# Stage B's score fills regrouped over both row halves of the array, and a changed rule for filling gaps in a planned schedule

## The chip, the cores and the metric

The kernel runs on one core of one Trainium2 chip. The metric is device time of the whole program in microseconds (us), the median of several runs. A core has five engines with queues of their own, which run in order and wait for one another by semaphores: TensorE (PE in the profile, with its weight loads as PEld), VectorE (DVE), ScalarE (ACT), GpSimd (POOL) and SyncE (SP, which here issues most of the transfers). TensorE's results go to tiles in PSUM, which this kernel allots in banks of 512 float32 columns in 128 partitions; ScalarE and VectorE read them there.

## What is computed

Two stages, one after the other, for each of 8 batches of 448 tokens.

```python
# stage A: attention of 12 heads of 64, with a soft cap on the scores
scores = cap * np.tanh(scale * (q @ k.T) / cap)      # cap = 30
attn = softmax(scores)
x = attn @ v                                         # 12 heads side by side: 768 columns
# stage B: 4 experts, each a causal attention of one head of 64 over x
logits = x @ w_gate                                  # each token takes its 2 best experts
for e in range(4):
    qe, ke, ve = x @ wq[e], x @ wk[e], x @ wv[e]
    a = softmax(where(causal, scale * (qe @ ke.T)))
    out += weight[:, e] * (a @ ve @ wo[e])           # weight is 0 where e isn't chosen
```

## The kernel before

**Tiling.** Heads go in pairs: two heads of 64 fill the 128 rows of the array, head 0 in rows 0 to 63 and head 1 in rows 64 to 127. There are 48 pairs, six to a batch. Scores stand transposed (keys in partitions, queries in columns), so that they serve as weights for the product with the values. The 448 keys are three chunks of 128 and a tail of 64. In stage B the experts go in pairs too, r = 0 for experts 0 and 1, r = 1 for 2 and 3; inside a pair the expert is e = 0 or 1 (also called g), with its `qe` and `ke` in rows 64e to 64e + 63.

**Stage A of a pair.** Four fills (`fill`, L444) put the scores of a chunk for both heads into a score buffer; the fourth, with the tails, is a single matmul of all rows (L449). ScalarE reads each by a tanh (`tanh`, L462, the instruction is L467): three of 896 columns and one of 448, called T0 to T3. Two exps (`expo`, L472; L474) follow on the tanh results, E0 of 1792 and E1 of 1344 columns. Then `a_pv_mm` multiplies by the values (L497 and L491, four parts in a plan), VectorE divides, and a transpose (`a_xt_tr`, L536) makes the batch's `xT`.

**Stage B of a batch.** Once the six pairs of a batch are in `xT`, the projections q, k (`b_qk`, in three parts of two matmuls) and v (`b_v`, in two) follow, then for each pair r two fills `b_fill(b, r, g)` (L675) and two exps `b_exp(b, r, g)` (L697, ScalarE at L703), named X0 and X1 below. Each works on a part of the score columns: before the change part g holds expert e = g, and part 0 has the tails of both experts besides. Causality cuts the blocks: chunk c of keys needs queries from 128c on, so its block has 448, 320 or 192 columns; the tail has 64. `COL` gives each block's column in the exp tile `pB`, which begins with 64 columns of zeros. After the exp GpSimd clears the upper triangle of each block on the diagonal (`affine_select`, L711). `b_pv` multiplies with the values for one expert, `b_ot` transposes, `b_wo` projects and `b_store` writes out.

**Two score buffers.** `ps_score` has two buffers of 1024 float32 (two banks each). T and X fills take turns in the order `reads`, so a fill may start when the ScalarE instruction two places earlier has read its buffer. Other PSUM tiles come from four single banks (`ps_aux`).

**The order of the work.** ScalarE's order is written out in `prog` (L894): for pair p it is T0, T1, E1 of the pair before, T2, T3, E0. In 14 of the 48 slots (`EXPB`, L891: two for each of the batches 0 to 6) stage B of an earlier batch comes in: T0, T1, X0, E1, X1, T2, T3, E0. TensorE's order comes from a planner, `Plan` (L18), which runs when the program is built and has no part in its execution. It keeps a clock for TensorE, VectorE and ScalarE; a unit of work has an estimated duration, dependencies and a due time. Before each fill, `do_fill` (L920) asks the planner to fill TensorE's time (`pump`, L86): no unit starts after `until`, when the fill's buffer comes free, and none is to end after `latest`, which is the time at which ScalarE will want the fill, less the fill's cost and 0.4 us. `step` (L65) finds the earliest possible start among the ready units, takes from those within 0.3 us of it the one that is due first, and emits it; in the kernel before, if that one doesn't end by `latest`, nothing more is placed in this gap. Some estimated durations: a half of `pv` 0.235 us (two parts make 0.47), `xt` 0.22, a part of `v` 0.33, of `q` or `k` 0.377, the transposes of a new pair (`tr`) 0.43, `pvB` 0.31, `wo` 0.33.

**The end.** The last batch, with whatever is left in the plan, is ordered by another planner (`last_batch`, L1026; `Graph.solve`, L150): a list schedule improved by 4000 random trials with a fixed seed, from the planner's clocks at that point.

Of the kernel before, what the change touches and what calls it, by code (L numbers as in the profile page):

```python
# [17 lines left out]
class Plan:  # L18
# [46 lines left out]
    def step(self, until, latest):  # L65


        at = {}
        for u in self.work:
            r = self.ready(u)  # L70
            if r is not None:
                at[u["key"]] = max(r, self.pe)
        if not at:
            return False
        first = min(at.values())
        u = min(
            (u for u in self.work if at.get(u["key"], 1.0e9) <= first + 0.3),
            key=lambda u: u["due"],
        )
        if first > until or first + u["pe"] > latest:  # L80
            return False
        self.work.remove(u)
        self.emit(u)
        return True
# [156 lines left out]
def kernel(  # L241
# [24 lines left out]
    KC, KM = 3, 384  # L266
# [403 lines left out]

    COL = {(0, 0): 64, (0, 1): 512, (0, 2): 832, (1, 1): 1024, (1, 2): 1344, (1, 0): 1536}

    def b_fill(b, r, g):  # L675
        s = st[b]
        qe = s["qe", r]
        ke = s["ke", r]
        sc = ps_score.tile([128, 1024], f32, name=f"sB{g}_{b}_{r}", tag="score")

        def block(e, o, ko, n, to):

            h = slice(64 * e, 64 * (e + 1))
            nc.tensor.matmul(  # L684
                sc[to : to + n, o : o + S - ko], ke[h, ko : ko + n], qe[h, ko:S], start=True,
                stop=True,
            )

        if g == 0:
            for e in range(2):  # L690
                block(e, 0, KM, TL, 64 * e)
        for (e, c), o in COL.items():
            if e == g:
                block(e, o - 1024 * g, 128 * c, 128, 0)
        s["sc", r, g] = sc

    def b_exp(b, r, g):  # L697

        assert b < 2 or ("pvB", b - 2, E - 1) in plan.done
        pb = pB[2 * (b % 2) + r]  # L700
        n = 1024 - 64 * g
        o0 = 64 + 1024 * g
        nc.scalar.activation(  # L703
            pb[:, o0 : o0 + n], st[b].pop(("sc", r, g))[:, 0:n], AF.Exp, scale=isc
        )
        blocks = [(o, 0, 128, 128) for (e, _), o in COL.items() if e == g]
        if g == 0:
            blocks += [(0, 0, 64, 64), (0, 64, 128, 64)]
        for o, r0, r1, n in blocks:
            blk = pb[r0:r1, 64 + o : 64 + o + n]  # L710
            nc.gpsimd.affine_select(  # L711
                out=blk, in_=blk, compare_op=ALU.is_ge, fill=0.0, base=0,
                pattern=[[1, n]], channel_multiplier=-1,
            )

    def b_pv_mm(b, e):
# [4 lines left out]
        for n in range(4):  # L721
            w = WIN[n]
            ops = []
            for c in range(KC):
                if 128 * c <= w:
                    ops.append((64 + COL[(g, c)] + w - 128 * c, s["vall"][:, c, e, :]))
            if n == 3:
# [182 lines left out]
    def dur(o):  # L910
        if o[0] == "S":
            return 0.0
        if o[0] == "X":
            return 0.9
        return 0.09 + 0.373 * (4 - o[2]) if o[0] == "E" else 0.055 + 0.373 * HALF[o[2]]

    def fill_dep(o):
        return (("tr", o[1]),) if o[0] == "T" else (("q", o[1], o[2]), ("k", o[1], o[2]))

    def do_fill():  # L920
        nonlocal nfill
        o = reads[nfill]
        rel = ends[nfill - 2] if nfill >= 2 else 0.0
        cost = 0.55 if o[0] == "X" else 0.5 if o[2] < KC else 0.19
        for d in fill_dep(o):
            plan.force(d)
        at = plan.act + sum(dur(x) for x in prog[pos : where[nfill]])
        plan.pump(rel, at - cost - 0.4)
        plan.pe = max(plan.pe, rel, *(plan.done[d] for d in fill_dep(o))) + cost
        fill(*o[1:]) if o[0] == "T" else b_fill(*o[1:])  # L930
        plan.done[("f", nfill)] = plan.pe + plan.LAT
        nfill += 1
# [10 lines left out]
    def slot(p):  # L943
# [24 lines left out]
        if p >= HP and p % HP == 0 and p < NP:  # L968
            batch(p // HP - 1)
# [10 lines left out]
    def batch(b):  # L980
        x = ("xt", HP * b + HP - 1)
        t0, t1 = nom["X", b, 0, 0], nom["X", b, 1, 0]
        for r, t in enumerate((t0, t1)):
            plan.parts(("q", b, r), 3, 1.13, 0.55, [x, ("w", ("q", r))], t - 4.0, b_qk, b, r, "q")
            plan.parts(("k", b, r), 3, 1.13, 0.55, [x, ("w", ("k", r))], t - 4.0, b_qk, b, r, "k")
        for n in range(4):
            d = [("v", b, n - 1)] if n else [x, ("w", "v")]
            plan.parts(("v", b, n), 2, 0.66, 0.6, d, t0 + 2.0 * n, b_v, b, n)
        plan.add(("g1", b), 0.0, 1.0, [("v", b, 3)], t1 + 1.0, b_gate, b, aux=None)
        plan.add(("g", b), 0.0, 0.8, [("g1", b), ("G", b)], t1 + 3.0, b_gate2, b, aux=None)  # L990
        for e in range(E):
            due = t1 + 6.0 + 3.0 * e
            d = [("X", b, e // 2, e % 2), ("g", b)] + [("pvB", b, e - 1)] * (e % 2)
            plan.add(("pvB", b, e), 0.31, 0.7, d, due, b_pv, b, e)
            if e % 2:
                plan.add(("oT", b, e // 2), 0.22, 0.35, [("pvB", b, e)], due, b_ot, b, e // 2)
        for n in range(4):
            for f in range(2):
                i = 2 * n + f
                d = [("oT", b, 1), ("w", "o")] if i == 0 else [("wo", b, *divmod(i - 1, 2))]  # L1000
                due = t1 + 19.0 + 1.5 * i
                plan.add(("wo", b, n, f), 0.33, 0.5, d, due, b_wo, b, n, f)
# [23 lines left out]
    def last_batch():  # L1026


        p, b = NP - 1, B - 1
        c = b - 1  # L1030
# [22 lines left out]
        BOTH = ("aux", "tail")  # L1053
# [4 lines left out]
        def op(key, eng, deps, fn, *args, group=None, groups=(), opens=None):  # L1058
            after = max([plan.done[d] for d in deps if d in plan.done], default=0.0)
            groups = (group,) if group else groups  # L1060
            f = (lambda e: fn(*args, e == "ACT")) if len(eng) > 1 else (lambda e: fn(*args))
            bias = 0.0
            if key[0] == "qk":
                bias = BR * (key[1] == 0)
            elif key[0] in ("pvL", "otL"):
                bias = BA * (key[1] == "A")
            elif key[0] == "sL":
                bias = BA * (key[1][0] == "A")
            elif key[0] in ("wo", "st"):
                bias = BA * (key[1] == b and key[2] < 2) - BW * (key[1] == c)  # L1070
            elif key[0] in ("pv", "xtp", "xt"):
                bias = BX
            G.op(key, eng, deps, f, groups, opens, after, bias)


        for u in (p - 1, p):
            for i in range(2):
                if ("pv", u, i) not in left and u < p:
                    continue
                g = ("pv", u, i)  # L1080
# [9 lines left out]
            g = ("xtp", u)  # L1090
# [18 lines left out]
        for e in range(E):  # L1109
            if ("pvB", c, e) in left:  # L1110
                g = ("pvB", c, e)
                r = e // 2
                op((*g, 0), {"PE": 0.31}, [("X", c, r, e % 2)], b_pv_mm, c, e, group=g, opens=BOTH)
                op((*g, 1), {"DVE": 0.18}, [(*g, 0)], b_pv_rc, c, e, group=g)
                op((*g, 2), {"DVE": 0.17}, [(*g, 1), ("gate", c, 8), ("g", c)], b_pv_sl, c, e)
                d = [(*g, 2)] + [("pvB", c, e - 1, 3)] * (e % 2)
                op((*g, 3), {"DVE": 0.43}, d, b_pv_osc, c, e, group=g)
        for r in range(2):
            if ("oT", c, r) in left:
                g = ("oT", c, r)  # L1120
                d = [("pvB", c, 2 * r + 1, 3)]
# [25 lines left out]
        for n in range(4):  # L1147
            for f in range(2):
                if ("wo", c, n, f) in left:
                    d = [[("oT", c, 0), ("oT", c, 1)]]  # L1150
# [42 lines left out]
        for r in range(2):  # L1193
            for w in "qk":
                g = ("qk", r, w)
                for j in range(NDC):
                    if (*g, j) in plan.done:
                        G.held[g] = "aux"
                        continue
                    d = [("xt", x0 + j)] + [(*g, j - 1)] * (j > 0)  # L1200
                    op(
                        (*g, j), {"PE": 0.19}, d, qk_mm, r, w, j, group=g,
                        opens=None if j else BOTH,
                    )
                d = [(*g, NDC - 1)] + [("el", NDC - 1)] * (r == 1 and w == "q")
                op((*g, "out"), both(0.6, 0.53), d, q_out if w == "q" else k_out, r, group=g)
        g = ("qk", 1, "q")
        for j in range(NDC):
            d = [("xt", x0 + j), (*g, 0)] + [("el", j - 1)] * (j > 0)
# [4 lines left out]
        for m in range(2):  # L1214
            g = ("vl", m)
            prev = None
            for j0, j1 in ((0, 3), (3, 5), (5, 6)):
                for i in range(2):
                    d = [("xt", x0 + j1 - 1), prev or ("xtp", p, 0)]
# [3 lines left out]
                        opens=BOTH if i + j0 == 0 else None,  # L1223
# [46 lines left out]
        for x, (blocks, o0) in BANKS.items():  # L1270
            rs = {a[0] for a in blocks}
            for e in range(2):
                o = o0 + (320 if x[0] == "C" else 384) * e
                for r, k0, q0, q1 in blocks:
                    if x[0] == "C" and k0 == TAIL:
                        o = o0 + 320 * e
# [4 lines left out]
            g = [("sL", x, e) for e in range(2)]  # L1281
# [4 lines left out]
            for e in range(2):  # L1286
                op(
                    ("sL", x, e), {"ACT": 0.49 if x[0] == "C" else 0.38}, [("sL", x, "mm")],
                    exps, x, e, group=g[e],
# [58 lines left out]
        for q in "AB":  # L1348
            need = {"A": (0,), "B": (0, 1)}[q]
            for r in range(2):  # L1350
                g = ("pvL", q, r)
                d = done[q, r] + [("vl", m, "out") for m in need]
# [8 lines left out]
            for n in (0, 1) if q == "A" else (2, 3):  # L1361
                for f in range(2):
                    d = [[("otL", q, r, 1)] for r in range(2)]
# [90 lines left out]
```

The softmax here doesn't subtract the row's maximum and nothing guards it: scores larger than these inputs give would overflow.

## Time and profile before

| what | value |
|---|---|
| time, median of 3 runs | 332.28 us (332.13 to 333.07) |
| span of the profiled execution | 330.7 us |
| mean granted TensorE clock | 0.984 |
| first tanh / end of the last exp of stage A | 8.23 us / 309.2 us |
| 144 tanh of 896 columns, mean | 978 ns |
| 48 exp of 1792, 48 exp of 1344, mean | 1762 ns, 1370 ns |
| 14 exp of 1024, 14 exp of 960 of stage B, mean | 1023 ns, 962 ns |
| 112 matmuls of stage B's scores | 18.3 us busy |

A row of the profile's groups gives the line, engine, operation and tile, the shape and count, then the busy time in us with the mean of one in ns, and behind the second bar the time for which its engine was idle just before, with what ended it. The timeline gives start and length in us; instructions of one line that follow each other are merged and counted (x5). Neighbouring records on one engine can overlap: a tanh of 978 ns is followed by the next after 797 ns. So the pace of ScalarE is read from start to start, not from the lengths.

### The profile page before, as it was taken

To read this page: it belongs to the slowest core of one execution; us is meant where nothing else is said; L and a number is where in the kernel's file an instruction comes from. 1 tells how busy PE (TensorE), PEld (TensorE's weight loads), DVE (VectorE), ACT (ScalarE), POOL (GpSimd) and SP (SyncE) were. 2 spreads that over 40 slices of the span, in tenths; PEclk is the share of its full clock that TensorE was granted. 3 is DMA by queue.
4 is the path that set the end of the run, shared out by engine and by line. 5 is a ranking of instruction groups with operands and counts; after the bars stand their busy time and mean duration, and the time that the engine had idled before them with its cause. 6 is when DMAs were issued, how large, how long until landed. Compare 5 with 4: busy or idle time off the path is not lost.

```text
span 330.7 us, 8813 instructions
## 1 busy us (share of the span) xinstructions
PE 279.7 (85%) x3335; PEld 177.4 (54%) x3335; DVE 212.2 (64%) x745; ACT 312.0 (94%) x353; POOL 156.0 (47%) x476
## 2 busy tenths in 40 slices
PE   5486589977889988998899889998798898898992
PEld 2254365555456564556655566556555565555861
DVE  4255445576557786668956688568855686646682
ACT  2989999999999999999999999999999999999592
POOL 3489999456707299765805285173912020022000
PEclk9999979999999999999999999999999999999997
DMA  7899999950363999477074903577003101120017
GB/s 165 214 247 246 216 222 233 211 116 3 87 177 88 285 264 258 145 195 179 3 217 158 287 13 108 156 216 192 3 7 138 24 3 50 50 71 3 2 74 261
DMA packets 65146, 46.19 MB, mean 140 GB/s; under 512 B 25872, under 2 KB 61584, under 8 KB 65104
## 3 DMA queue, kind: packets, MB, share of 16 engines
q1 hardware_dynamic: 54032, 43.58, 51.1%
q0 software_dynamic: 10512, 1.58, 6.7%
q8 instruction: 26, 0.43, 0.5%
q10 hardware_dynamic: 560, 0.48, 0.5%
q14 instruction: 16, 0.13, 0.1%
HBM read 36.19 MB, written 11.01 MB: 143 GB/s over the span
## 4 chain that ended last, share of the span: by engine, by line
ACT 81%; PE 7%; DMA 5%; POOL 3%; issue 1%; SPq 1%; DVEq 0%; ACTq 0%; POOLq 0%; DVE 0%
ACT y L467 38%; ACT p L474 35%; ACT pBs L703 8%; DMA ktf<-in_k_dram 3%; DMA kf<-in_k_dram 2%; PE wops L785 2%; POOL pBs L711 1%; PE vps L567 1%; PE kps L648 1%; PE qps L648 1%; POOL q L393 1%; PE pv L497 1%; POOL k L390 0%; POOL ktzs L389 0%; PE pvB L730 0%
## 5 line engine op out<-in xcount | busy, mean ns | idle before, releaser
L467 ACT ACTIVATE y<-s 128x896 f16<-128x896 f32 x192 | 152.7, 883 | 2.2 <-PE s L449 1.1
L474 ACT ACTIVATE p<-y 128x1792 f16<-128x1792 f16 x96 | 150.0, 1566 | 0.0
L711 POOL TENSOR_SCALAR_AFFINE_SELECT pBs<-pBs 128x128 f16<-128x128 f16 (+1 forms) x112 | 27.8, 278 | 123.6 <-ACT pBs L703 122.7
L453 PE MATMUL s<-qt,kt 64*128 64x448 f16 x288 | 52.5, 370 | 18.8 <-ACT y L467 14.5
L497 PE MATMUL pv<-v16s,p 128*128 128x65 f16 x1152 | 62.4, 196 | 5.9 <-ACT p L474 5.1
L497 PEld LDWEIGHTS <-p 128*128 128x128 f16 x1152 | 52.5, 99 | 24.7 <-issue 10.1
L453 PEld LDWEIGHTS <-kt 64*128 64x128 f16 x288 | 18.1, 94 | 47.8 <-issue 38.1
L511 DVE TENSOR_TENSOR xk<-pv,rc 128x256 f16<-128x256 f32 x96 | 40.6, 424 | 3.2
L491 PE MATMUL pv<-vtzs,p 128*128 128x130 f16 x192 | 42.0, 222 | 0.0
L507 DVE RECIPROCAL rc<-pv 128x4 f32<-128x4 f32 x96 | 17.1, 180 | 37.9 <-PE pv L491 37.0
L372 DVE COPY ob<-wops 128x384 f32<-128x384 f32 (+1 forms) x55 | 30.5, 554 | 9.1 <-PE wops L785 8.4
L785 PE MATMUL wops<-wo,oT 128*128 128x384 f16 x128 | 30.2, 326 | 0.0
L567 PE MATMUL vps<-wvg,xT 128*128 128x260 f16 (+1 forms) x192 | 29.8, 275 | 0.0
L703 ACT ACTIVATE pBs<-sB 128x1024 f16<-128x1024 f32 (+1 forms) x28 | 27.8, 992 | 0.7
L393 POOL CAST q<-qf 112x512 f16<-112x512 f32 x46 | 27.9, 607 | 0.0
L390 POOL CAST k<-kf 128x384 f16<-128x384 f32 x48 | 24.1, 502 | 6.8 <-DMA kf<-in_k_dram 3.9
L389 POOL CAST ktzs<-ktf 64x64 f16<-64x64 f32 x92 | 21.3, 232 | 9.1 <-DMA ktf<-in_k_dram 3.9
L684 PE MATMUL sB<-qe,ke 64*128 64x192 f16 (+2 forms) x112 | 18.3, 274 | 8.3 <-ACT y L467 4.7
L401 POOL CAST v16s<-vf 128x384 f16<-128x384 f32 x48 | 24.5, 510 | 1.2 <-DMA vf<-in_v_dram 1.0
L648 PE MATMUL qps<-xT,wq 128*128 128x448 f16 x96 | 24.9, 354 | 0.0
L648 PE MATMUL kps<-xT,wk 128*128 128x448 f16 x96 | 24.8, 353 | 0.0
L431 DVE COPY qt<-tps 128x384 f16<-128x384 f16 x48 | 16.8, 351 | 12.3 <-PE tps L421 12.3
(120 smaller groups left out, 456.7 us busy)
## 6 DMA issues: line engine op xcount, KB each, us to landing
qf<-in_q_dram SPq DMA_DIRECT2D x23, 448.0 KB, 5.6
out_dram<-ob SPq DMA_DIRECT2D x24, 384.0 KB, 2.9
kf<-in_k_dram SPq DMA_DIRECT2D x23, 384.0 KB, 6.4
vf<-in_v_dram SPq DMA_DIRECT2D x23, 384.0 KB, 5.8
ktf<-in_k_dram SPq DMA_DIRECT2D x46, 32.0 KB, 5.5
vtf<-in_v_dram SPq DMA_DIRECT2D x46, 32.0 KB, 5.1
out_dram<-ob SPq DMA_DIRECT2D x7, 192.0 KB, 2.9
qf<-in_q_dram ACTq DMA_DIRECT2D x2, 224.0 KB, 4.0
```

Source lines behind the costliest of these rows:

```text
L393: eng.tensor_copy(q16, qf.rearrange("p h (c d) -> p c h d", c=QC))
L453: nc.tensor.matmul(sc[:, g, 0:S], kt[r, 128 * (i + 1) : 128 * (i + 2)], qt[r, :], start=True, stop=True,)
L467: nc.scalar.activation(y[(p, g)][:, 2 * (i % 2) : 2 * (i % 2) + n, :], score.pop((p, i))[:, 0:n, 0:S], AF.Tanh, scale=isc / capf,)
L474: nc.scalar.activation(pt, y.pop((p, g)), AF.Exp, scale=capf)
L491: nc.tensor.matmul(pv[:, n, :, :], pt[:, 2, w : w + 128], vtz[p % 12], start=False, stop=True, skip_group_check=True,)
L497: nc.tensor.matmul(pv[:, n, g, :], pt[:, 2 * (c % 2) + g, w : w + 128], v16[p % 12][:, g, c, :], start=(n == 0 and c == 0 and g == 0), sto ...
L511: nc.vector.tensor_tensor(xt[p][:, 2 * i : 2 * i + 2, :, :], pv[:, :, :, 0:Dh], rc.broadcast_to((128, 2, 2, Dh)), ALU.mult,)
L567: nc.tensor.matmul(ps, xT[b][:, j, w : w + 128], wvg[:, j, 0 : ps.shape[1]], start=(j == 0 and first), stop=(j == NDC - 1), skip_group_che ...
L648: nc.tensor.matmul(ps, w2[r][:, j, :], xT[b][:, j, :], start=(j == 0), stop=(j == NDC - 1), skip_group_check=(b == B - 1),)
L703: nc.scalar.activation(pb[:, o0 : o0 + n], st[b].pop(("sc", r, g))[:, 0:n], AF.Exp, scale=isc)
L711: nc.gpsimd.affine_select(out=blk, in_=blk, compare_op=ALU.is_ge, fill=0.0, base=0, pattern=[[1, n]], channel_multiplier=-1,)
L785: nc.tensor.matmul(ps, st[b]["oT", r][:, w : w + 128], wo2[r][:, f * (D // 2) : (f + 1) * (D // 2)], start=(r == 0), stop=(r == 1),)
```

## The change

Part g of stage B's scores now holds both experts. Part 0 has the two blocks of chunk 0 (448 columns for each expert) and the two tails; part 1 has chunks 1 and 2 of both (320 and 192 columns for each). In each part one expert's blocks lie in the first bank of the score buffer and the other's in the second, and the matmuls of the two experts alternate, so that the two halves of the array's rows can work at once. Part 0 is now 960 columns and part 1 is 1024. The four `pvB` of a batch all wait for X1 of their pair, since X1 holds columns of both experts.

In the planner an X fill is reckoned at 0.45 us instead of 0.55, and `step` considers only units that end by `latest`; before, it chose first and gave up if the choice didn't fit.

```diff
@@ step
-            if r is not None:
+            if r is not None and max(r, self.pe) + u["pe"] <= latest:
                 at[u["key"]] = max(r, self.pe)
...
-        if first > until or first + u["pe"] > latest:
+        if first > until:
             return False
@@ columns
-    COL = {(0, 0): 64, (0, 1): 512, (0, 2): 832, (1, 1): 1024, (1, 2): 1344, (1, 0): 1536}
+    COL = {(0, 0): 64, (1, 0): 512, (0, 1): 960, (0, 2): 1280, (1, 1): 1472, (1, 2): 1792}
+    XCOL = (0, 960, 1984)
@@ b_fill
+        for c in (1, 2) if g else (0,):
+            for e in range(2):
+                block(e, COL[e, c] - XCOL[g], 128 * c, 128, 0)
         if g == 0:
             for e in range(2):
                 block(e, 0, KM, TL, 64 * e)
-        for (e, c), o in COL.items():
-            if e == g:
-                block(e, o - 1024 * g, 128 * c, 128, 0)
@@ b_exp
-        n = 1024 - 64 * g
-        o0 = 64 + 1024 * g
+        n = XCOL[g + 1] - XCOL[g]
+        o0 = 64 + XCOL[g]
...
-        blocks = [(o, 0, 128, 128) for (e, _), o in COL.items() if e == g]
+        blocks = [(o, 0, 128, 128) for (_, c), o in COL.items() if (c > 0) == g]
@@ do_fill
-        cost = 0.55 if o[0] == "X" else 0.5 if o[2] < KC else 0.19
+        cost = 0.45 if o[0] == "X" else 0.5 if o[2] < KC else 0.19
@@ batch
-            d = [("X", b, e // 2, e % 2), ("g", b)] + [("pvB", b, e - 1)] * (e % 2)
+            d = [("X", b, e // 2, 1), ("g", b)] + [("pvB", b, e - 1)] * (e % 2)
@@ last_batch
-                op((*g, 0), {"PE": 0.31}, [("X", c, r, e % 2)], b_pv_mm, c, e, group=g, opens=BOTH)
+                op((*g, 0), {"PE": 0.31}, [("X", c, r, 1)], b_pv_mm, c, e, group=g, opens=BOTH)
```

## The prediction

> **What bounds the kernel now.** I read the page first: busy shares, the chain of waits, the groups.
>
> ```profile
> PE 279.7 (85%) x3335; PEld 177.4 (54%) x3335; DVE 212.2 (64%) x745; ACT 312.0 (94%) x353; POOL 156.0 (47%) x476
> ACT y L467 38%; ACT p L474 35%; ACT pBs L703 8%; DMA ktf<-in_k_dram 3%; DMA kf<-in_k_dram 2%; PE wops L785 2%; POOL pBs L711 1%; PE vps L567 1%; PE kps L648 1%; PE qps L648 1%; POOL q L393 1%; PE pv L497 1%; POOL k L390 0%; POOL ktzs L389 0%; PE pvB L730 0%
> L703 ACT ACTIVATE pBs<-sB 128x1024 f16<-128x1024 f32 (+1 forms) x28 | 27.8, 992 | 0.7
> ```
>
> ScalarE (ACT) is busy for 94% and carries 81% of the chain with three instructions: tanh (L467), exp of stage A (L474), exp of stage B (L703). VectorE, GpSimd and the DMA queues matter only where they hold up ACT. The last row looks as if stage B's exp cost ACT 0.7 us of idle time in all, but records of neighbours on ACT overlap, so a wait can hide in an overlap that is missing. So I went to the timeline, ACT first around one of the 14 places where stage B's exp comes in:
>
> ```profile
> 210.99 1.04 ACT L467 ACTIVATE y<-s 128x896 f16<-128x896 f32 x1
> ...
> 211.79 1.05 ACT L467 ACTIVATE y<-s 128x896 f16<-128x896 f32 x1
> 212.91 1.02 ACT L703 ACTIVATE pBs<-sB 128x1024 f16<-128x1024 f32 x1
> 213.83 1.31 ACT L474 ACTIVATE p<-y 128x1344 f16<-128x1344 f16 x1
> ```
>
> Columns: start, duration. A tanh of 896 is followed by the next instruction after 0.80 (210.99 to 211.79), but the exp of stage B starts 1.12 after its tanh. The 14 starts of a first part (X0) in the timeline lie 1.15, 0.99, 1.07, 0.99, 1.13, 1.05, 1.12, 1.05, 1.12, 1.05, 1.13, 1.05, 1.13, 1.01 after their tanh: 15.02 in all, against 14 x 0.797 = 11.16 without a wait. So **3.87 us** are lost there. The second part (X1) follows the exp of 1344 after 1.21, as a tanh does: nothing is lost. Between 23 and 309 us I find no other stretch of ACT above its floor. What X0 waits for is on TensorE (PE):
>
> ```profile
> 211.45 0.22 PE L532 MATMUL xtp<-pswap,xk 128*128 128x128 f16 x1
> 212.09 0.73 PE L684 MATMUL sB<-qe,ke 64*64 64x64 f16 x5 [0.42 <-ACT y L467]
> 212.75 0.50 PE L785 MATMUL wops<-wo,oT 128*128 128x384 f16 x2
> 213.18 0.58 PE L684 MATMUL sB<-qe,ke 64*128 64x320 f16 x3
> ```
>
> The score buffers are two. The first tanh of the slot ends at 212.03 (210.99 + 1.04) and frees one; PE, idle for 0.42, starts the fill at 212.09, needs 0.73, and ACT starts 0.09 later. 0.24 + 0.06 + 0.73 + 0.09 = 1.12: the whole period is explained by the fill's length. X1's fill of 0.58 has the exp of 1344 beside it.
>
> **What the Trainium skill says.** "TensorEngine Tiling (Array Packing)", Tiling Modes (Key Properties): tiles of the array work independently, so row halves run at once, but a change of mode, not of tile, drains the array. The trace agrees with both. Stage A's fills, one matmul for each half, take 0.36 for the pair, and two pairs 0.55 at the least, so a pair costs about 0.20 where the mode stays:
>
> ```profile
> 58.09 0.59 PE L453 MATMUL s<-qt,kt 64*128 64x448 f16 x4
> 206.44 0.36 PE L453 MATMUL s<-qt,kt 64*128 64x448 f16 x2 [0.31 <-ACT y L467]
> 206.74 0.34 PE L532 MATMUL xtp<-perm,xk 128*128 128x128 f16 x3
> ```
>
> After the lone pair the next operation, of another mode, starts 0.30 later instead of 0.20: a switch costs some 0.10. The same page, Gotcha 1, says that row tiles that run at once must write different banks. That is the new layout: e = 0 in columns 0 to 511 of the buffer, e = 1 in 512 to 1023. No page is needed for the rest.
>
> **The change, part by part.** (1) *First fill.* Inside the old fill the five matmuls start at 0, 0.00, 0.149, 0.349, 0.485 and the last takes 0.243 (the mean of its form): two tails at once (64*64), then 448, 320 and 192 columns one after the other on one half. New: 448 of both halves at once, then the tails of both at once. The pair 448 to the next operation of another mode costs 0.296 (above), the tails take 0.20 (rows of 64x64: 200 ns), so 0.50; ends: 0.41 if the switch to 64*64 drains nothing, 0.73 if the halves did not overlap at all. I take 0.50, as the old fill shows the switch too (0.149 between starts for only 64 columns). It is 0.23 shorter. Taking 0.23 from each of the 14 excesses, none below zero, leaves 0.13, 0.04, 0.10, 0.02, 0.09, 0.03, 0.10, 0.02, 0.10, 0.02, 0.10 and three zeros: 0.76. **Gain on ACT 3.87 - 0.76 = 3.1 us** (3.8 at 0.41).
>
> (2) *Second fill.* 320 of both, then 192 of both: 0.14 + 0.24 = 0.39 for 0.58; hidden behind the exp of 1344 before and after. It frees PE only.
>
> (3) *Exp.* The parts have 960 and 1024 columns instead of 1024 and 960: 0.85 and 0.92 from start to next start either way. Nothing.
>
> (4) *Masks.* GpSimd did 5 selects after X0 and 3 after X1 (1.27 and 0.78 in the timeline at 227.42 and 229.49); now 4 and 4, about 1.0 each. It is idle around them (waits of 123 us in all for L703). Both pvB of a pair now wait for X1 and its four selects: masks are ready some 1.2 after X1 ends, 0.25 later than now, while the planner reckons 0.8. A pvB put right there would block PE, in order, with a stage A fill behind it, for up to 0.4. Stage A's fills lie beside an exp of 1.2 or 1.6 between release and use, which hides that; only the fill of T3 beside a tanh of 0.80 is tighter. I take 0; bound 7 x 0.3 = 2.1.
>
> (5) *Planner.* A gap before a fill is bounded by `until` (buffer free) and `latest`. With the order T0 T1 E T2 T3 E each stage A fill has an exp between, so latest lies over 1.0 after until and any unit that may start fits: the rule changes nothing there. It bites only in slots with stage B: before X0 (latest is 0.05 before until, formerly 0.15) and before T3 (0.21 after). So the first 58 us stay as they are, with the start's gaps. Before the 14 X0 fills PE idles 0.42 to 0.99 (sum 8.3); half an attention product (a part of `pv`, 0.235) or a transpose of 0.22 now goes into about half of them. The planner's buffer-free time is some 0.25 ahead of the real one, so a unit as planned does not delay X0. Effect on ACT 0.
>
> (6) *Tail.* The stretches:
>
> ```profile
> 250.00:309.20 59.20, 54.11 (x647) 33.74 (x646) 38.57 (x134) 58.93 (x64) 8.29 (x35) 1.00 0.12 42
> 309.20:325.00 15.80, 15.26 (x193) 10.51 (x190) 11.76 (x44) 11.20 (x28) 0.00 (x0) 1.00 0.27 90
> ```
>
> Columns: length, then busy PE, PEld, DVE, ACT, POOL. After the last exp PE is busy 15.26 of 15.80, so leftovers of batch 6 (three pvB, two transposes, eight projections) are paid there. In the last 22 us of ACT, two slots free 2 x (0.23 + 0.19) = 0.84 of PE, while ACT shortens by 0.44; net 0.4, plus up to 0.5 from filled gaps. I take **-0.4**. The tail's order comes out of a random search whose input changes, so I bound it by -1.2 and +1.5.
>
> Sum: 332.28 - 3.1 - 0.4 = **328.8 us**.
>
> **Rivals.** (A) The tails drain nothing, or more leftovers move ahead: 332.28 - 3.8 - 1.1 = 327.4. For it: PE backlog at the end; against: 0.149 in the old fill. (B) The tail's new order is worse by 1.5: 330.7. For it: the search; against: PE, which bounds it, has less to do. (C) Slower: units in the gaps wait in truth for VectorE (before five X0 fills the trace names VectorE's gate steps as last) or a pvB waits for the four selects, and the tightest fill stands behind them. 14 x 0.25 + 2.1 = 5.6 added: 334.4. Against: 0.42 or more of idle PE before each X0. (D) The halves don't overlap and order alone changes: 332.3. Against: every stage A fill.
>
> **Chances.** Forecast 0.68 (327.9 to 329.8), A 0.14, B 0.10, C 0.05, D 0.03. B stays faster by over 0.3% (below 331.28) but for a bit. Faster 0.90, same 0.04, slower 0.06. A range 327.2 to 330.7 leaves out about half of A, C, D and the end of B.
>
> **What would show it.** X0 should start 0.80 to 0.93 after its tanh; the first sB fill should last near 0.50 with starts 0, 0, 0.30, 0.30, the second near 0.39; ACT before the first X0 unchanged; the time from the last exp to the end near 21 us. A fill of 0.41 moves it to A. A first fill that starts more than 0.1 after its tanh ends, or idle time of ACT at L467 in slots with stage B, would be C.

## The result: faster by about 0.6%, with the fill as predicted and two terms of the sum off

The changed kernel takes 330.07 us (median of 5 runs, 328.92 to 330.68) against 332.28 before (331.46 to 333.07): ratio 0.9931, 95% interval 0.9904 to 0.9958. A second series of the same kernel, run with the experiments below, gave 330.46 against 332.18, ratio 0.9954 (0.9941 to 0.9967). The forecast was 328.8 in a range of 327.2 to 330.7: the direction and the range held, the gain was 2.2 us instead of 3.5. The time lies above the 327.9 to 329.8 in which the forecast itself was expected, on the side of rival B.

**Profile after.** The page first:

```profile
PE 275.5 (84%) x3335; PEld 175.8 (54%) x3335; DVE 213.9 (65%) x744; ACT 310.9 (95%) x354; POOL 155.6 (47%) x476
ACT y L467 38%; ACT p L474 37%; ACT pBs L705 7%; DMA ktf<-in_k_dram 3%; PE wops L787 2%; PE vps L567 2%; PE sB L686 1%; SPq L316 1%; POOL q L393 1%; POOL k L390 0%; POOL ktzs L389 0%; PE s L453 0%; PE kps L648 0%; PE xtp L532 0%; PE pvLB L1310 0%
L705 ACT ACTIVATE pBs<-sB 128x960 f16<-128x960 f32 (+1 forms) x28 | 29.2, 1042 | 0.0
```

ScalarE is still the bound; its exp of stage B (now L705) no longer shows idle time, and TensorE is busy for 4.2 us less. The same slot as before the change, ScalarE and then TensorE in the timeline (start, duration):

```profile
209.11 1.08 ACT L467 ACTIVATE y<-s 128x896 f16<-128x896 f32 x1
...
209.91 1.09 ACT L467 ACTIVATE y<-s 128x896 f16<-128x896 f32 x1
210.85 1.00 ACT L705 ACTIVATE pBs<-sB 128x960 f16<-128x960 f32 x1
211.72 1.35 ACT L474 ACTIVATE p<-y 128x1344 f16<-128x1344 f16 x1
```

```profile
210.24 0.51 PE L686 MATMUL sB<-qe,ke 64*128 64x448 f16 x4 [0.41 <-ACT y L467]
210.68 0.34 PE L532 MATMUL xtp<-perm,xk 128*128 128x128 f16 x3
...
211.34 0.39 PE L686 MATMUL sB<-qe,ke 64*128 64x320 f16 x4
```

The first fill lasts 0.51 us instead of 0.73, the second 0.39 instead of 0.58. X0 starts 0.94 after its tanh (it was 1.12). Over all 14 places X0 starts 12.75 us after its tanh in sum instead of 15.02.

The span went from 330.7 to 328.2 in the profiled runs. Cut at the start of the tanh before the first X0, at the end of the last stage A exp and at the end of the last copy out of PSUM:

| stretch | before | after | difference |
|---|---|---|---|
| start, up to the tanh before the first X0 | 60.32 | 59.65 | -0.67 |
| from there to the end of the last exp | 248.89 | 246.65 | -2.24 |
| from there to the last copy | 16.12 | 16.83 | +0.72 |
| last copy to the end (transfers) | 5.39 | 5.10 | -0.29 |

The first and the last row are taken as chance: TensorE's order up to the first X0 fill is the same in both kernels, and the same order gave starts between 59.65 and 62.2 in the runs below. What the change did is the middle: -2.24 + 0.72 = -1.5, close to the second series.

### The profile page after: what moved, and what is told of

The parts are those of the page before. It is cut to its first block, busy times and chain, and to the rows that moved or that the text cites. A ratio compares the mean times of both kernels' runs of the same rounds, so it can differ in the third digit from the quotient of the medians.

```text
span 328.2 us, 8804 instructions
## 1 busy us (share of the span) xinstructions
PE 275.5 (84%) x3335; PEld 175.8 (54%) x3335; DVE 213.9 (65%) x744; ACT 310.9 (95%) x354; POOL 155.6 (47%) x476
## 4 chain that ended last, share of the span: by engine, by line
ACT 83%; PE 8%; DMA 3%; POOL 2%; issue 2%; SPq 1%; DVE 0%; POOLq 0%
ACT y L467 38%; ACT p L474 37%; ACT pBs L705 7%; DMA ktf<-in_k_dram 3%; PE wops L787 2%; PE vps L567 2%; PE sB L686 1%; SPq L316 1%; POOL q L393 1%; POOL k L390 0%; POOL ktzs L389 0%; PE s L453 0%; PE kps L648 0%; PE xtp L532 0%; PE pvLB L1310 0%
## 5 line engine op out<-in xcount | busy, mean ns | idle before, releaser
L467 ACT ACTIVATE y<-s 128x896 f16<-128x896 f32 x192 | 156.7, 925 | 1.2 <-PE s L453 0.6
L474 ACT ACTIVATE p<-y 128x1792 f16<-128x1792 f16 x96 | 154.0, 1608 | 0.0
L497 PE MATMUL pv<-v16s,p 128*128 128x65 f16 x1152 | 63.5, 197 | 6.5 <-ACT p L474 5.8
L705 ACT ACTIVATE pBs<-sB 128x960 f16<-128x960 f32 (+1 forms) x28 | 29.2, 1042 | 0.0
L648 PE MATMUL kps<-xT,wk 128*128 128x448 f16 x96 | 24.1, 353 | 0.0
L406 POOL CAST vtzs<-vtf 64x64 f16<-64x64 f32 x96 | 22.8, 237 | 2.6
```

Source lines behind the costliest of these rows:

```text
L467: nc.scalar.activation(y[(p, g)][:, 2 * (i % 2) : 2 * (i % 2) + n, :], score.pop((p, i))[:, 0:n, 0:S], AF.Tanh, scale=isc / capf,)
L474: nc.scalar.activation(pt, y.pop((p, g)), AF.Exp, scale=capf)
L497: nc.tensor.matmul(pv[:, n, g, :], pt[:, 2 * (c % 2) + g, w : w + 128], v16[p % 12][:, g, c, :], start=(n == 0 and c == 0 and g == 0), sto ...
L648: nc.tensor.matmul(ps, w2[r][:, j, :], xT[b][:, j, :], start=(j == 0), stop=(j == NDC - 1), skip_group_check=(b == B - 1),)
L705: nc.scalar.activation(pb[:, o0 : o0 + n], st[b].pop(("sc", r, g))[:, 0:n], AF.Exp, scale=isc)
```

## The experiments

In all of them *stretch* is the second row of the table and *tail* the third. Two theories on the stretch stand against each other. **S**, which is the prediction's: ScalarE loses what X0's start comes too late, start to start. **E**, formed from the profile after: ScalarE's pace is that of its ends, and part of a late start is covered by work in flight.

### The planner's part alone

```diff
@@ on the kernel before: old COL, b_fill, b_exp; new rule in step
-        cost = 0.55 if o[0] == "X"
+        cost = 0.45 if o[0] == "X"
```

> The kernel before with the planner's part of the change alone (the rule and the cost of 0.45), old columns and fills. Theory 1 (the fill's length is all): the X0 fill stays at 0.73, the stretch from the tanh before the first X0 to the last exp stays at 248.9 us, and the tail is near that of the changed kernel (21.9 instead of 21.5): time 332.3 to 332.8. Rival (filled gaps are worth something of their own): stretch or tail shorter by 0.5 or more, time 331.0 to 331.8. Second rival (a unit in the gap blocks the X0 fill): stretch 249.5 or more, time 333 or more.

Measured: 332.26 us, ratio 0.9996 (0.9981 to 1.0012); stretch 248.91, first fills 0.73, tail 16.83. So the rule and the lower cost alone are worth nothing on ScalarE. But the tail is already the changed kernel's 16.83, before any change of the columns.

### The new columns with the old rule

```diff
@@ on the changed kernel: step
-            if r is not None and max(r, self.pe) + u["pe"] <= latest:
+            if r is not None:
...
-        if first > until:
+        if first > until or first + u["pe"] > latest:
```

> The changed kernel with the old rule in step (choose first, give up if it doesn't fit); columns, fills, waits and the cost of 0.45 as changed. Theory 1 (the gain is the fill's, the rule matters only for what the plan does at the end): the X0 fill lasts 0.51 and all 14 X0 end 0.86 after the tanh before them, so the stretch from the tanh before the first X0 to the last exp would be 246.7 us, but the planner itself reckons its ScalarE clock 3.1 us later at the end (307.5 against 304.4) and the tail 1.3 longer, so some fill near the end is late: stretch 248 to 250, time 332 to 334.5. Rival (the planner's clock doesn't tell what the chip does, and the rule is idle): stretch 246.7, time 330.0.

Measured: 332.61 us, ratio 1.0021 (1.0006 to 1.0037), stretch 248.33, tail 18.30. All fills have the new lengths, and the gain is gone. (The profiled execution was the longest of 22, 336.12 us; 3 us of that are in its start.) Nine of the 14 X0 take 0.86 from end to end as in the changed kernel, five don't: the first is 0.74 late (TensorE waited 1.50 for the transfer of `wq`, which also came late by chance in changed_again below), three are 0.18 late and the last 0.66. The timeline of TensorE ahead of one of the three:

```profile
187.51 0.55 PE L648 MATMUL qps<-xT,wq 128*128 128x448 f16 x2
187.90 1.30 PE L648 MATMUL kps<-xT,wk 128*128 128x448 f16 x6
189.92 0.99 PE L686 MATMUL sB<-qe,ke 64*128 64x448 f16 x8 [0.72 <-DVE ke L372]
```

The whole k projection stands right ahead of the fill that needs it, and TensorE then sits for 0.72 until VectorE has copied `ke`; both X fills (x8) follow at once. In the first profile of the changed kernel none of the 14 comes late. The four late fills other than the first cost 1.2 us together, and the tail is 1.47 longer than in the changed kernel: the larger part of the loss lies there. So the two parts are not independent: the rule with the lower cost is worth nothing on the old fills, and the rule some 2 us with the new ones (332.61 against 330.46). That the planner left the projection to the last moment because its parts were chosen and then didn't fit is what the code suggests; the trace shows only the resulting order. The old rule with the new columns and the old cost of 0.55 wasn't tried.

### A first fill shorter still

```diff
@@ b_fill (block takes the first query column as a further argument)
-            for e in range(2):
-                block(e, 0, KM, TL, 64 * e)
+            # one matmul of 64 query columns, 128 keys, row half 0
+            block(0, 0, KM - 64, 128, 0, KM)
```

> The changed kernel, but the two tail matmuls of the X0 fill (64x64 tiles of the array) are replaced by one of 64 columns in the mode of the 448 pair: the tails of the two experts' scores are then not computed right, which leaves the work of the other engines as it is. The fill should last 0.40 instead of 0.51 if the 0.30 between starts is the switch of mode. Theory E (ScalarE's pace is that of its ends; X0 already ends 0.86 after the tanh before it, which is its own length, so nothing is left to win): start to start X0 falls from 12.75 us in all to 11.6 or less, but the stretch from the tanh before the first X0 to the last exp stays at 246.65 within 0.1, time 330. Rival S (the pace is that of the starts, as the prediction had it): 14 X0 still lose 1.59 us in all, of which 1.1 to 1.5 go: stretch 245.2 to 245.6, time 328.7.

Measured: fill 0.375, stretch **246.649** (changed kernel 246.650), tail 16.83, time 329.52, ratio 0.9914 (0.9890 to 0.9937). The stretch is E's to the nanosecond, and the tail is the same; the 0.55 between the medians is left to the start and the transfers. E's number for the starts was a miss: they sum to 12.61, not 11.6. The timeline shows why:

```profile
209.60 2.03 ACT L467 ACTIVATE y<-s 128x896 f16<-128x896 f32 x2
211.34 1.15 ACT L704 ACTIVATE pBs<-sB 128x960 f16<-128x960 f32 x1
212.21 1.49 ACT L474 ACTIVATE p<-y 128x1344 f16<-128x1344 f16 x1
```

The pair of tanh spans 2.03 here and 1.89 in the changed kernel (209.11 to 211.00), at the same pace of starts. The fill gets its buffer when the first tanh *ends*, and every record is 0.14 longer: ScalarE merely starts earlier on what ends no earlier.

### A first fill made longer

```diff
@@ b_fill, ahead of the blocks; n = 224 or 448
+        if g == 0:
+            for e in range(2):
+                h = slice(64 * e, 64 * (e + 1))
+                nc.tensor.matmul(sc[0:128, 448 * e + 64 : 448 * e + 64 + n],
+                                 ke[h, 0:128], qe[h, 0:n], start=True, stop=True)
```

> The changed kernel, its order kept, with two more matmuls ahead of each X0 fill, one on each half of the rows, which write the first 224 of the 448 columns once before they are written for good: the fill should last 0.61 instead of 0.51. Theory E (ScalarE's pace is that of its ends; in the changed kernel X0's record starts 0.20 before the tanh ends in the first four slots and 0.14 in the last ten, and with a drained engine records overlap by 0.10, so 0.10 and 0.04 of a longer fill cost nothing): the 14 X0 take 12.04 + 4 x 0.00 + 10 x 0.06 = 12.6 us from end to end. Rival S (every ns of the fill is paid from start to start): 12.04 + 14 x 0.10 = 13.4 us.

> As fill_plus_224, with 448 columns written twice: the fill should last 0.71, nearly the 0.73 of the kernel before. Theory E: from end to end the 14 X0 take 12.04 + 4 x 0.10 + 10 x 0.16 = 14.0 us, 2.0 more than in the changed kernel, and the stretch from the tanh before the first X0 to the last exp is 248.65. Rival S: 12.04 + 14 x 0.20 = 14.8 us, stretch 249.45. If neither, and the stretch stays at 246.65, the fill's length was not the cause at all.

| | fill | 14 X0 end to end: E, S | measured | stretch | time, ratio |
|---|---|---|---|---|---|
| changed kernel | 0.51 | | 12.04 | 246.65 | 330.07, 0.9931 |
| with 224 columns more | 0.61 | 12.6, 13.4 | 12.69 | 247.43 | 330.33 (3 runs), 0.9934 (0.9909 to 0.9960) |
| with 448 columns more | 0.70 | 14.0, 14.8 | 14.00 | 248.75 | 331.56, 0.999 (0.997 to 1.001) |

S is out, twice. E's two thresholds (0.10 in the first four slots, 0.04 in the other ten) give both numbers. They differ because X0 starts 0.04 after the end of its fill in the first four slots and 0.10 in the others, where the trace has one more semaphore instruction of ScalarE before it; that this instruction is the reason wasn't tested. With 448 columns the fill is nearly the old one, in the new columns and the new order, and the old stretch of 248.89 is nearly back. The timeline at its X0:

```profile
210.61 1.85 ACT L467 ACTIVATE y<-s 128x896 f16<-128x896 f32 x2
212.51 0.97 ACT L712 ACTIVATE pBs<-sB 128x960 f16<-128x960 f32 x1
```

The tanh ends at 212.46, X0 starts 0.05 later and ends at 213.48: 1.02 from end to end, 0.16 more than the 0.86 of the changed kernel. (TensorE waits 0.40 before this fill too, so its length and nothing ahead of it is what counts.)

### The order in the tail

```diff
@@ on the changed kernel: step
-            (u for u in self.work if at.get(u["key"], 1.0e9) <= first + 0.3),
+            (u for u in self.work if at.get(u["key"], 1.0e9) <= first + 0.2),
```

> The changed kernel with step taking the most urgent of the units within 0.2 us (not 0.3) of the earliest, seed as it was. From the last 306 matmuls on TensorE's order is that of the kernel before, the fills are the changed ones. Theory 1 (the gain on ScalarE is the fill's and the loss in the tail is the order's): stretch 246.65, and from the last exp to the last copy 16.12 us as in the kernel before instead of 16.83; time 2.2 under the kernel before plus or minus 0.5, 0.7 under the changed one. Rival (the tail grew because of the new layout of the columns): 16.8.

> The changed kernel as it is, on the same chip as same_tail, for its time beside it and for what the profile repeats. Stretch from the tanh before the first X0 to the last exp 246.65, from the last exp to the last copy 16.83; the start up to that tanh (59.65 in the first profile, 59.65 to 60.3 in those with the same order up to there) and the way from the last copy to the end (5.10, in others 4.28 to 5.52) are left to the transfers and free to move. Time 330.0 plus or minus 0.6. If stretch or tail move by over 0.2, differences of that size between orders mean nothing.

Measured: same_tail 330.10 us, ratio 0.9939 (0.9915 to 0.9963), stretch 246.80, tail **16.12**. changed_again 330.46, 0.9954 (0.9941 to 0.9967), tail 16.83, stretch 246.93: it moved by 0.28, beyond the 0.2 that it was allowed, with the first X0 alone 0.36 late behind a wait of TensorE of 1.63 for `wq`. The tail stretches of the two (length, then busy PE, PEld, DVE, ACT, POOL):

```profile
306.78:322.90 16.12, 15.26 (x193) 10.52 (x190) 12.09 (x44) 11.20 (x27) 0.00 (x0) 1.00 0.29 94
```

```profile
309.15:325.99 16.84, 15.72 (x194) 10.61 (x194) 12.21 (x43) 11.67 (x29) 0.00 (x0) 1.00 0.30 102
```

The new columns have no part in the longer tail: with the old order of the last 305 matmuls it is the old one to the hundredth. The changed order has 0.46 more of TensorE's work after the last exp (15.72 against 15.26) and leaves TensorE idle for 0.26 more in all; its longest gap, of 0.46, stands before the last eight projections, where the old order has none (changed kernel, timeline):

```profile
320.38 0.22 PE L1338 MATMUL otLB<-swap,oscLB 128*128 128x128 f16 x1
321.06 1.47 PE L787 MATMUL wops<-wo,oT 128*128 128x384 f16 x8 [0.46 <-ACT oT L372]
```

ScalarE has two copies of projections in hand (319.92, 0.86 us) when the last transpose is ready, so the `oT` copy starts only at 320.67. By time, same_tail can't be told from the changed kernel beside it: 0.36 us between the medians, with overlapping intervals.

### Other orders

```diff
@@ step; near_first / near_two
-            (u for u in self.work if at.get(u["key"], 1.0e9) <= first + 0.3),
+            (u for u in self.work if at.get(u["key"], 1.0e9) <= first + 0.1),   # near_two: 0.2
@@ Graph.solve
-        rnd = random.Random(1)
+        rnd = random.Random(10)                                                 # near_two: 6
```

> The changed kernel with another plan: step takes the most urgent of the units within 0.1 us of the earliest instead of 0.3, and the search for the tail's order starts from another seed; the same instructions in another order. Theory 1 (the tail is bound by TensorE and by the order the search finds): the planner leaves 21 units instead of 26 to the tail and reckons it 0.75 shorter, ScalarE's stretch unchanged at 246.7: tail near 21.2, time 329.1 to 329.5. Rival (the tail's length is set by chip latencies that the search doesn't know): tail 21.9 plus or minus 0.3, time 330.

> The changed kernel with step taking the most urgent of the units within 0.2 us (not 0.3) of the earliest, and another seed for the tail's search: the same instructions in another order. The planner leaves 25 units to the tail instead of 26 and reckons the tail at 21.79 instead of 22.23. Theory 1 (the part of the tail up to the last copy follows the order, 16.12 us in the kernel before at a reckoned 21.98 and 16.83 in the changed one at 22.23): 15.9 to 16.2 here, ScalarE's stretch 246.65, so 0.6 to 0.9 under the changed kernel: 329.2 to 329.5. Rival (an order that differs brings a late fill somewhere, as in near_first): stretch 247 or more, time 330 or more.

> near_first once more, for its one late fill (X0 of the second slot, 0.64 us late at 74.2, where the trace shows TensorE at part of its clock). Theory 1 (the clock's dip hit by chance): no late fill, stretch 246.65, last exp to last copy 16.14, time 329.3. Rival (the order itself leaves TensorE idle there, the clock falls and the fill is late every time): late again by 0.4 or more, stretch 247.1 or more.

near_first: 330.09 us, ratio 0.9928 (0.9903 to 0.9952), tail 16.14 (21.2 up to the end of the program, as Theory 1 had it), but stretch 247.29, with the second X0 0.64 late. near_two: 329.51, 0.9919 (0.9894 to 0.9944), stretch 246.64, tail 16.58 and not the 15.9 to 16.2 that was expected: the planner's reckoning of the tail (21.79 against 21.98 for the old order, whose tail is 16.12) is no guide at this size. near_first_again: 330.27, 0.9943 (0.9923 to 0.9963), and the same X0 is late again, by 0.55. Stretches of near_first_again (after the busy times: granted TensorE clock, DMA share, GB/s):

```profile
70.00:72.00 2.00, 0.98 (x17) 0.73 (x16) 1.86 (x8) 2.00 (x4) 1.43 (x5) 1.00 0.00 0
72.00:74.00 2.00, 1.93 (x32) 1.52 (x30) 0.81 (x4) 2.00 (x3) 0.00 (x0) 0.74 0.00 0
74.00:76.00 2.00, 2.00 (x21) 1.36 (x19) 1.77 (x8) 1.56 (x3) 0.00 (x0) 0.50 0.04 8
76.00:78.00 2.00, 1.70 (x23) 1.02 (x20) 0.92 (x4) 2.00 (x3) 0.96 (x4) 0.91 0.00 0
```

TensorE is idle for half of 70 to 72, its clock is then down to 0.50, the same units take some 1.5 times as long, and the X0 fill behind them is late. "TensorE: Matmul & The Clock Gate" of the Trainium skill, Part 1, says that the clock halves after an idle window of some 3.4 us and recovers after a busy one; the 0.50 agrees, but TensorE was idle here for 0.74 at most at a time. Nor do two half idle microseconds explain it. The changed kernel has the same two ahead of its second X0, and keeps a clock of 1.00 after them:

```profile
68.54:70.54 2.00, 0.98 (x17) 0.73 (x16) 1.57 (x8) 2.00 (x4) 1.44 (x5) 1.00 0.29 74
70.54:72.54 2.00, 1.93 (x39) 1.45 (x37) 1.55 (x8) 2.00 (x3) 0.00 (x0) 1.00 0.00 0
```

The two orders differ over a longer stretch, the 3.4 us up to the same point (near_first_again, then the changed kernel):

```profile
68.60:72.00 3.40, 1.52 (x19) 1.01 (x19) 3.12 (x16) 3.40 (x6) 2.64 (x9) 1.00 0.09 23
```

```profile
67.14:70.54 3.40, 2.00 (x28) 1.46 (x28) 2.91 (x12) 3.40 (x6) 2.64 (x9) 1.00 0.51 143
```

Both profiles of this order have TensorE busy for 1.52 there and the fall of the clock behind it, so the order is the likely cause. Two profiles don't show it: in changed_again the clock fell to 0.50 between 86 and 89, where the first profile of the same kernel kept 1.00.

None of these versions beats the changed kernel by more than the runs can tell.

## Why the prediction was right, and where it was off

- **What bounds the kernel; what X0 waits for: right.** The fill's length set X0's start. Lengthening the fill brings the loss back in the size that E reckons, with all else in place.
- **Step 1, the fill: right.** 0.50 was predicted, 0.51 came; the tails start 0.295 after the pair, so the switch of mode costs what was read from stage A's fills. With one mode the third matmul starts after 0.188 and the fill takes 0.375. The rule of different banks that the prediction took from the skill isn't tested: no run puts the 448 columns of both halves into one bank. (The two tails do write one bank, in different partitions, and start 3 ns apart.) Rival D (halves don't overlap) is out.
- **Step 1, the gain: mis-sized.** "So 3.87 us are lost there" is the failed step. ScalarE ran 248.89 us where 246.65 was possible, so 2.24 were lost, not 3.87. All of it came back; the 0.76 that was to remain as a loss is none. The error is in the yardstick: 0.797 from start to start is not ScalarE's pace, though the section on the profile before says that pace is read so. A tanh of 896 ends 0.807 after the one before it. With each tanh the starts run some 10 ns further ahead of the ends, so records lengthen as long as nothing stalls. The timeline of the changed kernel:

```profile
25.17 1.73 ACT L467 ACTIVATE y<-s 128x896 f16<-128x896 f32 x2
...
42.01 1.83 ACT L467 ACTIVATE y<-s 128x896 f16<-128x896 f32 x2
...
58.85 1.94 ACT L467 ACTIVATE y<-s 128x896 f16<-128x896 f32 x2
```

  Two tanh of the same work take 1.73, 1.83, 1.94: the overlap of the first with the second grows from 0.13 to 0.34. A late X0 first eats this lead, and only what is beyond it delays an end. By ends, X0 took 1.031 in the first four slots of the kernel before and 1.091 in the others (in the slot that the prediction shows, from 212.84 to 213.93), where 1024 columns need 0.913 (X1 of the changed kernel): 4 x 0.118 + 10 x 0.178 = 2.25. The starts of X0 did not move by 3.1 either, but by 2.27 (15.02 to 12.75): the 14 fills are 3.02 shorter, but each gets its buffer at the end of the first tanh of its slot, and these records are 0.67 longer in sum. "ScalarE: Activation LUTs" of the Trainium skill (What ACT_TABLE_LOAD costs) has neighbours overlap by some 93 ns; here it is 0.10 just after a stall and up to 0.34 later, and the measurement decides.
- **Steps 2 and 3: right.** 0.39 as predicted and hidden. By ends the two exps take 0.86 and 0.91, in either order.
- **Step 4, masks: right.** 1.02 and 1.03 for the selects after X0 and X1; TensorE's weight loads for `pvB` wait 0.6 us in all for GpSimd, against 0.7 before.
- **Step 5, planner: right for the chip, short on the reason.** TensorE's first 448 matmuls keep their order, its idle time before the X0 fills falls from 8.3 us to 7.3, and the rule with the lower cost gives 0.9996 on the old fills. But "effect on ACT 0" holds only on the old fills; layout_only shows that without the rule the new fills come late.
- **Step 6, tail: wrong in sign.** -0.4 was taken, +0.72 came. The step assumed that time saved on TensorE moves leftovers ahead. The planner left one part of the k projection more to the tail, and the search put a wait of 0.46 before the last projections. That is rival B at half its size, which was given 0.10; it is a matter of order alone (same_tail, planner_only).
- **The sum.** -3.1 and -0.4 were taken, -2.24 and +0.72 came, and chance in the start and the transfers added -0.96 in the profiled pair. So part of the nearness of 330.07 to the forecast is luck; the second series is nearer to what the change is worth.

## What to carry to other kernels

Before pricing a wait on a saturated engine, measure the engine's pace from end to end as well as from start to start; where records overlap by a growing amount, only what is left after the overlap is used up can be won, and a wait shortened beyond that wins nothing. When the work of an array half is regrouped, count the switches of its mode with the columns. Where a planner writes the order, a part of a change that is worth nothing alone can be what keeps another part's gain, and any change of its input re-rolls the tail: set the tail's order apart before judging the rest.

## What the runs showed of the hardware

- The starts of ScalarE's tanh records, which read PSUM, run ahead of their ends: start to start 0.797, end to end 0.807 for 896 columns, 0.423 and 0.433 for 448. The exps of stage A, which read SBUF, show no such gain (1.587 and 1.585 for 1792). A late operand cuts this overlap back, to 0.10 us where it stalls ScalarE (the version with 448 columns more); it reached 0.34 in the changed kernel and 0.48 in the version with the tails in one mode.
- A switch between 64x128 and 64x64 tiles costs about 0.10 us of TensorE: behind a pair of 448 columns the next matmul starts after 0.295 with it and after 0.188 without (the version with the tails in one mode).
- TensorE's clock fell to 0.50 without a long idle time: behind 3.4 us with TensorE busy for 1.52 and no gap above 0.74, in both profiles of one order. Behind 2.00 of the same 3.4 us it stayed at 1.00.
- From the last copy to the end of the program the same order took between 4.29 and 5.10 us, more than the tail's orders differ.
